# A retention, routing and two-MLP kernel: every routing product with a stationary operand of 128 columns and 128 rows

## The chip, the core and the metric

The kernel runs on one core of a Trainium2 chip. The metric is the device time of one execution in microseconds (us), lower is better. The time shown of a kernel is the median of several executions; the profile is of one further execution, whose own time stands beside it.

Engines: PE (TensorE, matrix products), PEld (the loads of PE's stationary operand, which may run ahead of the products), DVE (VectorE), ACT (ScalarE), POOL (GpSimd), SP (SyncE, which here issues DMAs and loads one register per expert).

## What is computed

Three stages follow each other: a retention layer (attention with a decay instead of a softmax), a mixture of eight experts with a greedy capacity, and a dense MLP. The cut reference:

```python
# retention: B, H, S, D = 4, 8, 576, 64
scores = scale * np.matmul(q, k.transpose(0, 1, 3, 2))
ret = scores * Dmat[None]                  # gamma[h] ** (i - j) for i >= j
x = (ret @ v) as [2304 tokens, 512]
# routing: 8 experts, capacity 288 tokens each
logits = x @ w_gate
for idx in np.argsort(-logits.flatten()):
    tok, e = idx // 8, idx % 8
    if assigned[tok] >= 0 or counts[e] >= 288: continue
    assigned[tok] = e; counts[e] += 1
# experts, F = 1024
out[mask_e] = np.maximum(x[mask_e] @ w1[e], 0) @ w2[e]
# dense MLP, DFF = 2048
h = x @ w_in; g = h * np.tanh(softplus(h)); return g @ w_out
```

## The kernel before, in words

**Retention** (`attention`) goes over 18 tiles of 128 tokens. PE, DVE and POOL follow an order written by hand; SP loads `qk` and `kv` of a tile (512 KB each) three tiles ahead. The constants come by a few DMAs between the first loads; one of them is `cst` (L273), which holds the 128x128 identity and a triangle. POOL fills the constants of the routing at the start (`routing_setup`).

**Routing.** The greedy assignment is done expert by expert: in each of eight rounds the expert is found that is filled first, and the logit (threshold) at which it is. The threshold is found digit by digit in six steps over the 32-bit key (`route`, L427 to L450). In a step with m candidates (m is 63, 63, 31, 31, 31, 32) DVE writes marks `G` (L427; tokens on 128 partitions, 18 tiles by 64 columns, m of them used), PE adds up 18 products `pF` with `G[:, t, :m]` as the stationary operand and the one-hot choice `oh` (8 columns) as the moving one (L445), DVE compares with the capacity (`sat`, L366), PE multiplies with `digit` (L450, m rows by 128 columns), and DVE takes the maximum (L411) and goes on to the next step. A step of the first round's first digit stands in L305. After six steps two small products (`before` and `oneb`, 128x128, L474 and L475) number the chosen tokens.

Then `tokens` builds the list of the expert's tokens: DVE writes a one-hot matrix `ohb` (L587, 18 tiles by 96 columns) in two halves of nine tiles, PE multiplies each half by `R` (18 products `pI`, 96 columns stationary, 6 moving, L595), DVE turns the sums into indices (`chosen`, L599), and POOL gathers the rows with indirect DMAs. The rows are transposed on PE (`mmx`, L628) and split into high and low parts.

**Experts** (`experts`): per expert 96 products `mma` and 96 `mmb` of 128x288 (L771), each value as a sum of three products of split parts. While the products of expert i run, the rounds of the next ones go on. **Order**: from the first round's second step on, a planner (`run_tasks`) chooses the order of PE, DVE, POOL, ACT and SP in the program with costs and priorities written into the `yield` lines; on the chip every engine then runs its list in that order and waits with semaphores. So six times there is a batch of 18 routing products on PE between two runs of `mma` or `mmb`. In the first round there are no expert products yet, and PE fills some of its waiting time with `warm` products (L781). The weights of `w_in` and `w_out` are converted piece by piece on ACT, DVE and POOL in the same stretch (`narrow`, tiles `words`, `dw`).

**Dense MLP** (`tiles`): six tiles of 384 tokens, `mmc` (L987) and `po` (L1048), until the end.

Of the kernel before, what the change touches and what calls it, by code (L numbers as in the profile page):

```python
# [17 lines left out]
P = 128  # L18
# [63 lines left out]
FC, FCN = _layout([("ident", P), ("tri", P)])  # L82
# [6 lines left out]
def constants():  # L89
    p = np.arange(P)  # L90
    f = np.zeros((P, FCN), np.float32)
    f[:, FC["ident"]] = np.eye(P)
    f[:, FC["tri"]] = p[:, None] <= p[None, :]
# [30 lines left out]
    return {"consts": f, "decays": d, "masks": m.reshape(P, 2, -1), "rconsts": r, "iconsts": c}  # L124
# [8 lines left out]
class Kernel:  # L133
# [3 lines left out]
    def attention(self):  # L137
# [6 lines left out]
        cst = persist.tile([P, FCN], F32, name="cst")  # L144
        self.ident = ident = cst[:, FC["ident"]]
        self.tri = cst[:, FC["tri"]]
        self.L = L = persist.tile([P, NT, E], F32, name="L")
        with ExitStack() as st:
# [124 lines left out]
            nc.sync.dma_start(cst, a["consts"])  # L273
# [21 lines left out]
            G = self.rw.tile([P, NT, 64], BF16, name="G")  # L295
            self.chosen = self.rw.tile([GB, E, 3], I32, name="chosen", bufs=1)
            pF = self.psum("pF", [64, E])
# [16 lines left out]
    def routing_setup(self):  # L314
# [14 lines left out]
        nc.gpsimd.memset(self.open, 1.0)  # L329
        self.tok = pr.tile([P, NT], I32, name="tok")  # L330

    def routing_consts(self):
# [8 lines left out]
        nc.vector.tensor_tensor(self.before, self.tri, self.ident, op=ALU.subtract)  # L341

# [14 lines left out]

    def reached(self, choice, G, ts):

        m, n = WIDTHS[0], ts.stop - ts.start  # L360
        self.nc.vector.tensor_tensor(G[:, ts, :m], choice[0][:, ts, None].to_broadcast([P, n, m]),
                                     self.rc[:, None, RC["first"]].to_broadcast([P, n, m]), op=ALU.is_ge)

    def saturated(self, pF, m):
        sat = self.rw.tile([64, E], BF16, name="sat")
        self.nc.vector.tensor_scalar(sat[:m], pF[:m, :], float(CAP), None, op0=ALU.is_ge)  # L366
        return sat

    def route(self):
# [8 lines left out]
        for i in range(E):  # L378
# [26 lines left out]
            for s in range(6):  # L405
                m = WIDTHS[s]
                if s or i:
# [18 lines left out]
                    G = rw.tile([P, NT, 64], BF16, name="G")  # L426
                    v.tensor_tensor(G[:, :, :m], key[:, :, None].to_broadcast([P, NT, m]),  # L427
# [15 lines left out]
                    pF = self.psum("pF", [64, E])  # L443
# [666 lines left out]
```

## Time and profile before

| | |
|---|---|
| median of 3 runs | 813.99 us (812.19 to 814.79) |
| the profiled execution | 809.8 us, its span 808.0 us |
| PE busy | 766.4 us, 95% of the span |
| DVE busy | 668.5 us, 83% |
| ACT, POOL busy | 413.2 us and 464.4 us |
| granted PE clock over the span | 0.98 of full |

Stages of the span: retention 0 to 84 us, the first round of the routing 84 to about 104 us, waiting for the first weights and rows until 125 us, experts with the other rounds 125 to about 340 us, the last expert and the start of the dense MLP 340 to 460 us, the dense MLP to 808 us.

How to read the rows: a line of a timeline is start, duration, engine, line, operation, output<-inputs, shapes and count; in square brackets the idle time of the engine just before and what ended it. A row that merges several instructions (x18) goes from the start of the first to the end of the last. A line of a window table is its length, then busy us and number of instructions of PE, PEld, DVE, ACT and POOL, then the granted clock of PE (1.00 is 2.4 GHz, 0.50 is 1.2 GHz), the busy share of the DMA engines, and GB/s. Starts on PE are when the instruction is handed to the array, so that what costs time in a dense stretch is the distance from one start to the next.

### The profile page before, as it was taken

How to read it: one execution, taken by the hardware profiler on the slowest of the kernel's cores; microseconds unless marked ns; L12 is line 12 of the kernel's file. 1: busy time of each engine (PE TensorE's matmuls, PEld its weight loads, DVE VectorE, ACT ScalarE, POOL GpSimd, SP SyncE). 2: the span in 40 equal slices, each digit the busy share in tenths (PEclk: the TensorE clock that was granted, in tenths of full speed). 3: DMA queues.
4: the chain of work that ended last, by engine and by line, in shares of the span. 5: the costliest groups of instructions: out<-in, count | busy, mean ns of one | idle time of the engine just before them, and what ended most of it. 6: DMA issues, size and time to landing. Idle time of an engine off the chain costs nothing.

```text
span 808.0 us, 16171 instructions
## 1 busy us (share of the span) xinstructions
PE 766.4 (95%) x6184; PEld 688.3 (85%) x6184; DVE 668.5 (83%) x1089; ACT 413.2 (51%) x781; POOL 464.4 (57%) x402
## 2 busy tenths in 40 slices
PE   7999479999999999799899899999999999999996
PEld 5898338898999989799898788898899988999985
DVE  2444687897988888696698999989998998998993
ACT  1233115556555565575664455555556556555552
POOL 3653035779797796340166776657466566655644
PEclk9999789999999999899999999999999999999999
DMA  9993165888888887986700010001001001000001
GB/s 342 408 354 129 41 208 184 265 264 283 252 290 251 299 265 229 331 270 231 247 1 21 20 40 21 12 21 47 2 20 40 19 21 40 20 1 13 27 1 39
DMA packets 61117, 112.52 MB, mean 139 GB/s; under 512 B 4848, under 2 KB 33008, under 8 KB 61040
## 3 DMA queue, kind: packets, MB, share of 16 engines
q1 hardware_dynamic: 44816, 74.00, 26.8%
q10 hardware_dynamic: 13248, 28.06, 10.4%
q0 software_dynamic: 2976, 9.44, 3.6%
q8 instruction: 48, 0.79, 0.4%
q14 instruction: 29, 0.24, 0.1%
HBM read 88.93 MB, written 22.54 MB: 138 GB/s over the span
## 4 chain that ended last, share of the span: by engine, by line
PE 59%; DVE 8%; DMA 2%; POOL 2%; issue 2%; ACT 1%; SPq 0%; POOLq 0%; ACTq 0%; DVEq 0%
PE mmc L987 23%; PE po L1048 21%; PE mmb L771 7%; PE mma L771 7%; DVE q L1017 2%; DMA st<-w 1%; PE pF L445 1%; DVE hl L797 1%; DVE ohb L587 1%; DVE wlo L560 1%; DVE G L427 1%; DMA st<-w_out 1%; POOL n L1019 1%; POOL gl L1029 1%; DVE n L1012 1%
## 5 line engine op out<-in xcount | busy, mean ns | idle before, releaser
L1017 DVE RECIPROCAL q<-q 128x384 f32<-128x384 f32 x96 | 244.3, 2545 | 11.3 <-ACT q L1015 9.7
L1019 POOL TENSOR_TENSOR n<-n,q 128x384 f32<-128x384 f32 x96 | 99.3, 1034 | 140.3 <-DVE q L1017 137.7
L1029 POOL TENSOR_TENSOR gl<-n,gh 128x384 fp32r<-128x384 f32 x96 | 105.4, 1098 | 50.5 <-ACT gh L1027 50.1
L987 PE MATMUL mmc<-yl,whi 128*128 128x384 f32 x384 | 130.2, 339 | 4.3 <-POOL yl L947 2.5
L987 PE MATMUL mmc<-yh,whi 128*128 128x384 f32 x384 | 130.0, 339 | 0.6 <-ACT yh L944 0.5
L987 PE MATMUL mmc<-yh,wlo 128*128 128x384 f32 x384 | 129.7, 338 | 0.0
L560 POOL TENSOR_TENSOR wlo<-st,whi 128x1024 fp32r<-128x1024 f32 x49 | 116.9, 2400 | 13.1 <-ACT whi L557 12.4
L1048 PE MATMUL po<-whi,gh 128*128 128x512 f32 x288 | 114.0, 396 | 0.0
L1048 PE MATMUL po<-whi,gl 128*128 128x512 f32 x288 | 113.9, 395 | 0.0
L1048 PE MATMUL po<-wlo,gh 128*128 128x512 f32 x288 | 113.3, 393 | 0.0
L1005 ACT ACTIVATE s<-mmc 128x384 f32<-128x384 f32 x96 | 47.1, 491 | 122.2 <-PE mmc L987 119.2
L1012 DVE SCALAR_TENSOR_TENSOR n<-s 128x384 f32<-128x384 f32 x96 | 103.3, 1076 | 2.1 <-ACT s L1005 1.2
L557 ACT CAST whi<-st 128x1024 fp32r<-128x1024 f32 x80 | 82.0, 1043 | 40.5 <-DMA st<-w 31.6
L771 PE MATMUL mma<-xh,whi 128*128 128x288 f32 x256 | 77.5, 303 | 3.0 <-DVE xl L620 3.0
L987 PEld LDWEIGHTS mmc<-yl,whi 128*128 128x128 f32 x384 | 72.1, 188 | 9.5 <-POOL yl L947 3.4
L771 PE MATMUL mmb<-hl,whi 128*128 128x288 f32 x256 | 77.9, 304 | 0.0
L771 PE MATMUL mmb<-hh,whi 128*128 128x288 f32 x256 | 77.4, 302 | 0.0
L771 PE MATMUL mmb<-hh,wlo 128*128 128x288 f32 x256 | 77.3, 302 | 0.0
L987 PEld LDWEIGHTS mmc<-yh,whi 128*128 128x128 f32 x384 | 72.1, 188 | 5.5 <-ACT yh L944 1.5
L771 PE MATMUL mma<-xh,wlo 128*128 128x288 f32 x256 | 76.7, 300 | 0.0
L771 PE MATMUL mma<-xl,whi 128*128 128x288 f32 x256 | 76.6, 299 | 0.0
L987 PEld LDWEIGHTS mmc<-yh,wlo 128*128 128x128 f32 x384 | 72.2, 188 | 0.0
(146 smaller groups left out, 1541.2 us busy)
## 6 DMA issues: line engine op xcount, KB each, us to landing
st<-w SPq DMA_DIRECT2D x64, 512.0 KB, 5.7
qk<-qk SPq DMA_DIRECT2D x18, 512.0 KB, 7.9
kv<-kv SPq DMA_DIRECT2D x18, 512.0 KB, 8.1
std<-w_out ACTq DMA_DIRECT2D x15, 512.0 KB, 5.1
std<-w_in ACTq DMA_DIRECT2D x14, 512.0 KB, 5.3
x_scratch<-xs SPq DMA_DIRECT2D x18, 256.0 KB, 4.1
y_scratch<-y ACTq DMA_DIRECT2D x32, 144.0 KB, 3.9
yt<-y_scratch SPq DMA_DIRECT2D x22, 192.0 KB, 2.4
```

The costliest lines, as they stand in the source:

```text
L427: v.tensor_tensor(G[:, :, :m], key[:, :, None].to_broadcast([P, NT, m]), T[:, None, :].to_broadcast([P, NT, m]), op=ALU.is_ge)
L445: nc.tensor.matmul(pF[:m, :], G[:, t, :m], oh[:, t, :], start=(t == 0), stop=(t == NT - 1))
L557: self.nc.scalar.copy(dst[0], st)
L560: (self.nc.vector if lo.engine == DVE else self.nc.gpsimd).tensor_tensor(dst[1], st, dst[0].bitcast(F32), op=ALU.subtract)
L771: self.nc.tensor.matmul(bank[1][:, :CAP], al if h == 2 else ah, bl if h == 1 else bh, start=(first and j == h == 0), stop=(last and j == n ...
L987: self.nc.tensor.matmul(bank[1][:, :TILE], (wl if h == 2 else wh)[:, c, cs], x[c][h == 1], start=(c == h == 0), stop=(c == HP - 1 and h == 2))
L1005: nc.scalar.activation(s, p, AF.Sigmoid)
L1012: v.scalar_tensor_tensor(u, s, 2.0, s, op0=ALU.subtract, op1=ALU.mult)
L1017: v.reciprocal(q, q)
L1019: nc.gpsimd.tensor_tensor(u, u, q, op=ALU.mult)
L1029: nc.gpsimd.tensor_tensor(gl, u, gh.bitcast(F32), op=ALU.subtract)
L1048: nc.tensor.matmul(po[j], (gl if h == 2 else gh)[:, js], (wl if h == 1 else wh)[:, f % 2], start=(f == h == 0), stop=(f == DFF // P - 1 an ...
```

## The change

Each stationary operand of a routing product becomes 128 columns and 128 rows:

- `G` is now one of two fixed tiles of 18 x 64 + 64 columns, filled with zeros once and used in turn (`marks_of`). The product of tile t reads columns 64 t to 64 t + 128: its own 64 and those of tile t + 1. Beyond its own m marks it reads marks of the next tile or of earlier steps; the surplus rows of `pF` (now 128) hold sums that nothing needs.
- `sat` is compared over 128 rows; `digit` has 128 rows and is zero beyond m, so that the surplus counts nothing.
- `ohb` is a fixed tile with 32 more columns (zero). The product of tile t reads columns 96 t to 96 t + 128; the surplus rows of `pI` are not read.
- `ident` and `tri` become two DMAs instead of one (`cst`).
- The costs of the planner stay as they are, and so does the order of the instructions on each engine after the start.

```diff
-        pF = self.psum("pF", [64, E])
+        pF = self.psum("pF", [P, E])
...
-                nc.tensor.matmul(pF[:WIDTHS[0], :], G[:, i, :WIDTHS[0]], choice[2][:, i, :], start=(i == 0), stop=(i == NT - 1))
-            self.first_step = choice, self.saturated(pF, WIDTHS[0])
+                nc.tensor.matmul(pF, G[:, i * 64:i * 64 + P], choice[2][:, i, :], start=(i == 0), stop=(i == NT - 1))
+            self.first_step = choice, self.saturated(pF)
...
-        self.digit = pr.tile([64, 6, P], BF16, name="digit")
+        self.digit = pr.tile([P, 6, P], BF16, name="digit")
+        nc.gpsimd.memset(self.digit, 0.0)
         for i, s in enumerate(SHIFTS):
-            nc.gpsimd.memset(self.digit[:, i, :], float(2 ** s))
+            nc.gpsimd.memset(self.digit[:WIDTHS[i], i, :], float(2 ** s))
...
+        self.G = [self.rw.tile([P, NT * 64 + 64], BF16, name=f"G{i}", bufs=1) for i in range(2)]
+        self.ohb = self.rw.tile([P, NT * GB + P - GB], BF16, name="ohb", bufs=1)
+        for g in self.G:
+            nc.gpsimd.memset(g, 0.0)
+        nc.gpsimd.memset(self.ohb[:, NT * GB:], 0.0)
...
+    def marks_of(self):
+        self.G.reverse()
+        return self.G[0]
...
-        sat = self.rw.tile([64, E], BF16, name="sat")
-        self.nc.vector.tensor_scalar(sat[:m], pF[:m, :], float(CAP), None, op0=ALU.is_ge)
+        sat = self.rw.tile([P, E], BF16, name="sat")
+        self.nc.vector.tensor_scalar(sat, pF, float(CAP), None, op0=ALU.is_ge)
...
-                        nc.tensor.matmul(pF[:m, :], G[:, t, :m], oh[:, t, :], start=(t == 0), stop=(t == NT - 1))
+                        nc.tensor.matmul(pF, G[:, t * 64:t * 64 + P], oh[:, t, :], start=(t == 0), stop=(t == NT - 1))
...
-                nc.tensor.matmul(pD, self.digit[:m, s, :], sat[:m], start=True, stop=True)
+                nc.tensor.matmul(pD, self.digit[:, s, :], sat, start=True, stop=True)
...
-                nc.tensor.matmul(pI, ohb[:, t], R[:, t].rearrange("p g c -> p (g c)"), start=(t == 0), stop=(t == NT - 1))
+                nc.tensor.matmul(pI, self.ohb[:, t * GB:t * GB + P], R[:, t].rearrange("p g c -> p (g c)"), start=(t == 0), stop=(t == NT - 1))
...
-            nc.sync.dma_start(cst, a["consts"])
+            nc.sync.dma_start(self.ident, a["ident"])
+            self.tri = one.tile([P, P], F32, name="tri")
+            nc.sync.dma_start(self.tri, a["tri"])
```

Two places show what moves. The first is PE in the sixth round (the list of the fifth expert after the first), from the ninth product of the first half of `ohb` to the start of the second half; three expert products `mma` stand between the halves. LDWEIGHTS is the load of the stationary operand, and in brackets is what it waits for. Before:

```order
L595 LDWEIGHTS ohb
L595 MATMUL pI_4746<-R,ohb 96x6
L771 MATMUL mma_4731<-xh,whi 128x288
L771 MATMUL mma_4731<-xl,whi 128x288
L771 MATMUL mma_4731<-xh,wlo 128x288
L595 LDWEIGHTS ohb [waits DVE_49]
```

With the change, the same place:

```order
L603 LDWEIGHTS ohb [waits DVE_49]
L603 MATMUL pI_4713<-R,ohb 128x6
L779 MATMUL mma_4698<-xh,whi 128x288
L779 MATMUL mma_4698<-xl,whi 128x288
L779 MATMUL mma_4698<-xh,wlo 128x288
L603 LDWEIGHTS ohb
```

The order is the same; the wait for DVE's second half of `ohb` moved from the tenth load to the ninth, since the ninth now reads 32 columns of tile nine, and with that ahead of the three expert products. The same is so in all eight rounds.

The second place is the start of SP's list, the DMAs of constants and first tiles; `DMAHW` is one of eight semaphores that the DMAs take in turn, each waiting for the one eight before it. Before:

```order
L272 DMA both<-both 128x288
L273 DMA cst<-consts 128x256
L174 DMA qk<-qk 128x1024 [waits DMAHW0_49]
L176 DMA kv<-kv 128x1024 [waits DMAHW1_49]
L275 DMA mask_83<-masks 128x1024 [waits DMAHW2_49]
L174 DMA qk<-qk 128x1024 [waits DMAHW3_49]
```

With the change:

```order
L266 DMA both<-both 128x288
L267 DMA ident<-ident 128x128
L269 DMA tri<-tri 128x128 [waits DMAHW0_49]
L168 DMA qk<-qk 128x1024 [waits DMAHW1_49]
L170 DMA kv<-kv 128x1024 [waits DMAHW2_49]
L271 DMA mask_83<-masks 128x1024 [waits DMAHW3_49]
```

There is one DMA more, of the same bytes in all, and the loads of tile 2 and the next ones wait for a DMA that was issued one place later.

## Rows read from the trace of the kernel before

**Rows 1.** The page's part 4, the chain of work that ended last.
```profile
PE 59%; DVE 8%; DMA 2%; POOL 2%; issue 2%; ACT 1%; SPq 0%; POOLq 0%; ACTq 0%; DVEq 0%
```

**Rows 2.** Window table: one cycle of an expert in the middle.
```profile
250.00:284.00 34.00, 33.95 (x338) 31.48 (x336) 29.22 (x95) 19.86 (x34) 27.91 (x16) 1.00 0.85 276
```

**Rows 3.** Window table: a piece of the first round.
```profile
92.00:94.00 2.00, 0.61 (x17) 0.45 (x17) 1.43 (x6) 0.00 (x0) 0.00 (x0) 0.50 0.00 0
```

**Rows 4.** Timeline of PE in the first round: a batch of 63 columns, one of 31.
```profile
90.76 1.12 PE L445 MATMUL pF<-oh,G 128*63 128x8 bf16 x18 [2.53 <-DVE known L432]
...
93.56 0.65 PE L445 MATMUL pF<-oh,G 128*31 128x8 bf16 x18 [1.26 <-DVE known L432]
```

**Rows 5.** Groups by shape, PEld, 90 to 102 us: count, busy us, mean ns, idle before.
```profile
L445 PEld LDWEIGHTS <-G 128*31 128x31 bf16 x54 | 1.7, 104 | 4.9 <-DVE known L432 4.9
L445 PEld LDWEIGHTS <-G 128*63 128x63 bf16 x18 | 1.0, 155 | 2.6 <-DVE known L432 2.6
...
L450 PEld LDWEIGHTS <-digit 31*128 31x128 bf16 x3 | 0.3, 98 | 0.1
```

**Rows 6.** Timeline, 103.2 to 104.4 us: two products with 128x128 in a row.
```profile
103.80 0.16 PE L474 MATMUL pP<-scan,before 128*128 128x2 bf16 x1 [2.24 <-DVE scan L471]
103.80 0.10 PEld L475 LDWEIGHTS <-oneb 128*128 128x128 bf16 x1 [2.21 <-issue]
103.83 0.16 PE L475 MATMUL pP<-scan,oneb 128*128 128x1 bf16 x1
```

**Rows 7.** Groups by shape, PEld, 125 to 303 us.
```profile
L445 PEld LDWEIGHTS <-G 128*31 128x31 bf16 x288 | 8.2, 94 | 3.6 <-DVE steps L437 2.3 <-DVE known L432 1.2
L445 PEld LDWEIGHTS <-G 128*63 128x63 bf16 x180 | 6.6, 114 | 2.4 <-DVE G L427 1.4 <-DVE known L432 1.0
...
L475 PEld LDWEIGHTS <-oneb 128*128 128x128 bf16 x5 | 0.5, 100 | 0.0
```

**Rows 8.** Timeline of PE, sixth round: the two halves of ohb, then batches.
```profile
280.32 0.53 PE L595 MATMUL pI<-R,ohb 128*96 128x6 bf16 x9
...
281.25 0.57 PE L595 MATMUL pI<-R,ohb 128*96 128x6 bf16 x9
281.67 0.38 PE L771 MATMUL mmb<-hh,whi 128*128 128x288 f32 x1
...
282.49 0.75 PE L445 MATMUL pF<-oh,G 128*63 128x8 bf16 x18
283.17 0.40 PE L771 MATMUL mmb<-hl,whi 128*128 128x288 f32 x1
...
290.10 0.61 PE L445 MATMUL pF<-oh,G 128*31 128x8 bf16 x18
290.63 0.40 PE L771 MATMUL mmb<-hl,whi 128*128 128x288 f32 x1
```

**Rows 9.** Timeline of DVE at the same place.
```profile
280.14 1.05 DVE L587 TENSOR_TENSOR ohb<-sc,rc 128x864 bf16<-128x864 f32 x1
281.11 1.33 DVE L427 TENSOR_TENSOR G<-sc,rc 128x1134 bf16<-128x1134 f32 x1
...
283.63 0.75 DVE L740 SCALAR_TENSOR_TENSOR dw<-std,ic,words 128x512 uint32<-128x512 uint32 x1
284.29 0.17 DVE L411 TENSOR_REDUCE sc<-pD 128x1 uint32<-128x8 f32 x1
...
286.64 0.14 DVE L432 TENSOR_TENSOR known<-known,sc 128x1 uint32<-128x1 uint32 x1
```

**Rows 10.** Timeline of PE in the eighth round: the second half of ohb.
```profile
319.53 0.57 PE L595 MATMUL pI<-R,ohb 128*96 128x6 bf16 x9
```

**Rows 11.** Timeline of DVE in the eighth round.
```profile
319.39 0.75 DVE L737 TENSOR_SCALAR words<-words,ic 128x512 uint32<-128x512 uint32 x1
320.13 0.16 DVE L599 TENSOR_REDUCE chosen<-pI 96x3 int32<-96x6 f32 x1
```

**Rows 12.** Timeline of POOL at the start.
```profile
1.90 0.90 POOL L324 MEMSET digit<- 64x128 bf16 x6
...
11.83 1.04 POOL L187 TENSOR_TENSOR ks<-kv,dec 128x512 f32<-128x512 f32 x1 [8.69 <-DMA kv<-kv]
```

**Rows 13.** Window table: the DMAs at the start.
```profile
8.00:10.00 2.00, 0.50 (x20) 0.26 (x12) 1.46 (x3) 0.00 (x0) 0.00 (x0) 1.00 1.02 406
```

More of the change, by code (lines that the diff above doesn't have):

```diff
@@ L79, in _layout @@
     return out, o
-FC, FCN = _layout([("ident", P), ("tri", P)])
 DC, DCN = _layout([("gk", NT * H), ("gs", NT * HP), ("gq", HP * P)])
@@ L90, in constants @@
     p = np.arange(P)
-    f = np.zeros((P, FCN), np.float32)
-    f[:, FC["ident"]] = np.eye(P)
-    f[:, FC["tri"]] = p[:, None] <= p[None, :]
     gamma = 1.0 - 2.0 ** (-5.0 - np.arange(H, dtype=np.float64))
@@ L143, in attention @@
         self.sc = self.right.enter_context(tc.tile_pool(name="sc", bufs=1, space=PSUM, side="right")).tile([P, 512], F32, name="sc")
-        cst = persist.tile([P, FCN], F32, name="cst")
-        self.ident = ident = cst[:, FC["ident"]]
-        self.tri = cst[:, FC["tri"]]
+        self.ident = persist.tile([P, P], F32, name="ident")
         self.L = L = persist.tile([P, NT, E], F32, name="L")
@@ L294, in attention @@
             self.psum = lambda name, shape: ps.tile(shape, F32, name=name, tag="pS" if name == "pF" else "pA", bufs=1 if name == "pF" else 2)
-            G = self.rw.tile([P, NT, 64], BF16, name="G")
+            G = self.marks_of()
             self.chosen = self.rw.tile([GB, E, 3], I32, name="chosen", bufs=1)
-            pF = self.psum("pF", [64, E])
+            pF = self.psum("pF", [P, E])
             early, late = slice(0, t - 1), slice(t - 1, NT)
@@ L425, in route @@
                         T = Tu[:, :m].bitcast(F32)
-                    G = rw.tile([P, NT, 64], BF16, name="G")
-                    v.tensor_tensor(G[:, :, :m], key[:, :, None].to_broadcast([P, NT, m]),
+                    G = self.marks_of()
+                    v.tensor_tensor(G[:, :NT * 64].rearrange("p (t m) -> p t m", m=64)[:, :, :m], key[:, :, None].to_broadcast([P, NT, m]),
                                     T[:, None, :].to_broadcast([P, NT, m]), op=ALU.is_ge)
@@ L442, in route @@
                     at = yield PE, 90 + 17 * m, [at], 0
-                    pF = self.psum("pF", [64, E])
+                    pF = self.psum("pF", [P, E])
                     for t in range(NT):
-                        nc.tensor.matmul(pF[:m, :], G[:, t, :m], oh[:, t, :], start=(t == 0), stop=(t == NT - 1))
+                        nc.tensor.matmul(pF, G[:, t * 64:t * 64 + P], oh[:, t, :], start=(t == 0), stop=(t == NT - 1))
                     at = yield DVE, 155, [at], 0
-                    sat = self.saturated(pF, m)
+                    sat = self.saturated(pF)
                 at = yield PE, 105, [at], 0
                 pD = self.psum("pD", [P, E])
-                nc.tensor.matmul(pD, self.digit[:m, s, :], sat[:m], start=True, stop=True)
+                nc.tensor.matmul(pD, self.digit[:, s, :], sat, start=True, stop=True)
             at = yield DVE, 2100, [at], 0
@@ L581, in tokens @@
         v.tensor_scalar(R[:, :, :, 1], g, self.rc[:, RC["base"]][:, NT:], None, op0=ALU.mult)
-        ohb = rw.tile([P, NT, GB], BF16, name="ohb", bufs=1)
+        ohb = self.ohb[:, :NT * GB].rearrange("p (t b) -> p t b", b=GB)
         halves = [slice(0, NT // 2), slice(NT // 2, NT)]
@@ L598, in tokens @@
         with nc.allow_low_precision(reason="small integers"):
-            v.tensor_reduce(idx, pI.rearrange("p (g c) -> p g c", c=2), AX.X, ALU.add)
+            v.tensor_reduce(idx, pI[:GB].rearrange("p (g c) -> p g c", c=2), AX.X, ALU.add)
         self.banks[nI] = self.listed[i] = at
```

7 lines of the change are left out of this document (4 added, 3 removed).

## The prediction

> **What bounds the kernel now.** I read the chain of waits first, then a table of windows, then timelines of PE and DVE around the lines that the diff touches. The chain is PE for 59% of the span and DVE for 8% [rows 1]; it can be followed back only to 199 us. In a cycle of one expert PE is busy 33.95 of 34 us at the full clock of 2.4 GHz [rows 2]. So from 125 to 318 us a product that costs PE less is worth its time, unless DVE holds the next step back. The first round of the routing (84 to 104 us) is something else: PE and DVE wait for each other, nothing runs beside it, and the granted clock there is 0.50, that is 1.2 GHz [rows 3]. There each ns of a batch lies on the path.
>
> **What a load of 128 columns costs.** This decides the sign, so I take it first. In a batch of 18 load and product pairs, PE is paced by the loads: at 1.2 GHz the batch of 63 columns takes 1.12 us, that of 31 columns 0.65 us [rows 4]. The durations of the loads follow: 104 ns for 31 columns, 155 for 63, but 98 for `digit`, which has 128 columns already [rows 5]. At 2.4 GHz it is 94, 114 and, for `oneb` with 128 columns, 100 ns [rows 7]. And at 1.2 GHz the products of `before` and `oneb` start at 103.80 and 103.83 us with the load of `oneb` between them, and the second takes no longer than the first [rows 6]. So in bf16 a load of 128 columns costs what one of 31 does, and one of 63 columns costs more. I take a batch of 128 columns at the 31-column one's price. `digit` had that price with 31 rows, so its new rows bring nothing.
>
> A rule of the Trainium skill bears on this: "TensorE: Matmul & The Clock Gate", section "Weight-path perf modes — Fast Weight Load (FWL) and DoubleRow", states that a load of exactly 128 columns that is not fp32 is read in wider pieces over four paths, in theory four times as fast for fp8 (of bf16 it puts two elements in a piece), and measured about twice as fast on trn2. The trace agrees with four rather than with two; the rival below with half the gain is what two would give. The same page, section "LDWEIGHTS (loading the stationary operand)", speaks against the change: its formula, columns / 1.2 ns, knows no such exception and makes the load of 128 columns about 107 ns; by that every batch gets longer, which is the last rival.
>
> **The change part by part.** (1) *First round.* One batch of 63 columns goes from 1.12 to 0.65 us: **-0.47 us**. The other batch of 63 (L305) stood mostly beside DVE's work, its last two products are worth some 0.05 us. The four batches of 31 and 32 columns stay. What follows (the first weights and rows) is waited for from here, so this lasts. Between -0.55 and -0.4.
>
> (2) *Batches of the later rounds.* At 2.4 GHz a batch of 63 costs 283.17 - 282.49 = 0.68 us of PE, one of 31 columns 290.63 - 290.10 = 0.53 us [rows 8]: -0.15 us for each of the two batches in a round, nothing for the other four.
>
> (3) *The list of tokens.* Nine products of 96 columns cost 281.67 - 281.25 = 0.42 us [rows 8]; at the 31-column price, 0.53 / 18 = 0.03 each, they cost 0.27. But the first half now waits at its ninth product for DVE's second half of `ohb`, and behind it stand the expert products that used to fill that time. In the row, DVE ends that half at 280.14 + 1.05 = 281.19 [rows 9] and PE starts the second half at 281.25, just in time. With the change PE starts the first half at 280.32, is through eight pairs at 280.56, and stands still for 0.69 us until 281.25. Then come the ninth pair (0.03), the three expert products that stood between (281.25 - 280.32 - 0.42 = 0.51 us), and the second half (0.27): 282.06 instead of 281.67, so **+0.4 us** instead of -0.3. The pattern is the same in five rounds (the third to the seventh); in the second and the eighth two products stand between and it is +0.3; in the first, `warm` products stand there and it costs nothing.
>
> (4) *What of (2) and (3) reaches the end.* In the same cycle DVE goes from 280.14 to 286.78 without a pause that PE could shorten: `ohb`, `G`, the conversion steps `words` and `dw`, the maximum at 284.29, the next `G`, `known` [rows 9]; PE starts the second batch of 63 right behind that. So PE, late by 0.4, loses a small wait of 0.1 before the first batch (`G` ends at 282.44, PE starts at 282.49), saves 0.15 in it and is 0.15 late after it; DVE wants the result only at 284.29, behind `dw`, so that this hides; a wait of some 0.05 before 286.78 goes too; and the second batch saves 0.15. The 31-column batches that follow are PE's own and unchanged. Sum of a round: +0.4 - 0.1 - 0.15 - 0.05 - 0.15 = **about 0**. Bounds: -0.15 (the late half hides wholly, only the batch behind `known` gains) to +0.4 (nothing is gained back), for the five rounds -0.75 to +2.0. The second round (PE +0.3 and -0.3) 0, from -0.3 to +0.3.
>
> (5) *Eighth round.* `chosen` starts when `words` ends, at 320.13, while the second half ends at 319.53 + 0.57 = 320.10 [rows 10, 11]. PE starts that half some 0.5 us later (the ninth pair and two expert products come first) and ends it 0.15 sooner: `chosen` **+0.3 us**, and behind it in DVE's list the splits that free the places for the last expert's weights. Between 0 and +0.4.
>
> (6) *Start.* POOL writes 768 columns of zeros, two times 1216 and 32. By `digit`, 0.90 us for 768 columns [rows 12], this is 3.8 us more; POOL then waits 8.69 us for the load of a `kv` tile anyway. **0**; without that cover it would be 3.8. SP issues the loads of tile 2 and the next ones a place later. The DMAs run at 406 GB/s with a busy share of 1.02 meanwhile [rows 13], so that bytes, not the time of issue, set when they land: **0**, at most one load of 512 KB, 1.3 us. `sat` over 128 rows instead of 63 stays one instruction of 8 columns: 0, and not above its 0.15 us.
>
> Sum: -0.47 + 0 + 0.3 = -0.2 us. On the profiled execution of 809.8 us that is 809.6; this execution lies 4.2 us below the median of the runs, 814.0, and on that scale the forecast is **813.8 us**. From the bounds: -0.55 - 0.75 - 0.3 = -1.6 and -0.4 + 2.0 + 0.3 + 0.4 + 1.3 = +3.6, so 812.4 to 817.6, and with the spread of a run (812.19 to 814.79, that is 1.3) 811.1 to about 818.
>
> **The rivals.** *Half the gain* (slower): a load of 128 columns in a stream costs what one of 64 does; single loads in the rows could hide that by running ahead. The batches of 63 then gain nothing, those of 31 and 32 columns lose. First round: 4 x 0.47 = 1.9 us. Six later rounds: 4 batches x 0.15 = 0.6 each on PE, 3.6 us. The wait at the ninth product is then not gained back: +0.4 in five rounds, 0.3 in two, 2.6. Together +8.1: **822 us**. It becomes slower than no change where a 128-column load in a batch costs over about 3 ns more than a 31-column one. Against it: 98 against 104 ns, and 155 for 63 columns at the same clock [rows 5].
>
> *No wait, all gained* (faster): the ninth product doesn't hold PE, and what PE saves all reaches the end: -0.5, 12 batches x 0.15 = -1.8, 14 halves x 0.15 = -2.1, together -4.4: **809.6 us**. For it: PE is dense [rows 2]. Against it: the order has the wait in every round, and DVE ends only 0.06 us before PE's start of the second half [rows 8, 9].
>
> *It doesn't do what it says* (slower by far): 128 columns take the time of 128 columns. From 31 to 63 columns a pair at 1.2 GHz gets longer by (1.12 - 0.65) / 18 / 32 = 0.8 ns for a column, at 2.4 GHz by (0.68 - 0.53) / 18 / 32 = 0.26 ns. First round: 4 x 18 x 97 x 0.8 ns + 18 x 65 x 0.8 ns = 6.5 us; six rounds of 4 x 18 x 97 x 0.26 + 2 x 18 x 65 x 0.26 ns = 2.4 us, 14.5 us, and the wait of 2.6: about +24, **838 us**. The load of `digit` speaks against it.
>
> **How the numbers follow.** A measurement of this kernel can tell 0.3%, 2.4 us, from no change. The forecast has 0.78, half the gain 0.11, all gained 0.08, not what it says 0.03. Faster: 0.08 and a little of the forecast's low end, 0.10. Slower: 0.11 + 0.03 and 0.04 of the forecast's high end, 0.18. Same: 0.72. The range goes from 809.5 (it takes in most of "all gained") to 818; left out are most of the two slow rivals and the tails, under 0.2.
>
> **What the profile after would show.** A batch of what was 63 columns in the first round at 0.65 us, at full clock 0.53 from start to start, the batches of 31 unchanged: (1) and (2). PE idle for 0.4 to 0.7 us ahead of the ninth product of each first half, ended by DVE `ohb`: (3). The second batch of each round still started by `known`: (4). I am wrong if the batches that had 31 columns get longer, if POOL or the loads of tile 2 come late at the start, or if the idle time at the ninth product shows up at the end of a cycle.

## The result and the profile after

The changed kernel takes **806.46 us** (median of 6 runs, 804.62 to 810.0), the kernel before 813.15 in the same comparison (6 runs): ratio 0.991, 95% interval 0.9887 to 0.9932. That is 6.7 us faster, where 813.8 us and no measurable difference was forecast, and below the lower end of the range. The profiled execution took 804.62 us, its span is 802.9 us, 5.1 less than the 808.0 before.

The first round went as forecast. PE's two batches of [rows 4] and the loads of marks of [rows 5]:

```profile
90.76 0.64 PE L453 MATMUL pF<-oh,G 128*128 128x8 bf16 x18 [2.53 <-DVE known L440]
...
93.10 0.64 PE L453 MATMUL pF<-oh,G 128*128 128x8 bf16 x18 [1.27 <-DVE known L440]
```

```profile
L453 PEld LDWEIGHTS <-G 128*128 128x128 bf16 x90 | 2.8, 105 | 9.6 <-DVE known L440 9.6
```

The batch of 63 columns went from 1.12 to 0.64 us, and the next one starts 0.46 earlier (93.56 before). At the full clock, the loads from 125 to 298 us (the place of [rows 7]) take 96 ns instead of 94 and 114:

```profile
L453 PEld LDWEIGHTS <-G 128*128 128x128 bf16 x558 | 16.0, 96 | 8.7 <-DVE known L440 5.9 <-DVE G L435 1.1
...
L603 PEld LDWEIGHTS <-ohb 128*128 128x128 bf16 x90 | 3.3, 96 | 5.6 <-DVE ohb L595 5.1
```

What was not forecast shows in the dense rounds. First PE's timeline of the kernel **before** in the sixth round, around one `digit` product (an expert product by itself starts 0.13 us after the one ahead):

```profile
283.67 0.30 PE L771 MATMUL mmb<-hl,whi 128*128 128x288 f32 x1
283.90 0.18 PE L450 MATMUL pD<-sat,digit 63*128 63x8 bf16 x1
284.00 0.40 PE L771 MATMUL mmb<-hh,wlo 128*128 128x288 f32 x1
284.24 0.29 PE L771 MATMUL mmb<-hh,whi 128*128 128x288 f32 x1
```

And **after**, the list of tokens, a `digit` product and a batch of marks in the same round (the place of [rows 8]):

```profile
275.56 0.35 PE L603 MATMUL pI<-R,ohb 128*128 128x6 bf16 x8
276.89 0.18 PE L603 MATMUL pI<-R,ohb 128*128 128x6 bf16 x1 [0.97 <-DVE ohb L595]
276.93 0.38 PE L779 MATMUL mma<-xh,whi 128*128 128x288 f32 x1
...
277.41 0.38 PE L603 MATMUL pI<-R,ohb 128*128 128x6 bf16 x9
277.65 0.38 PE L779 MATMUL mmb<-hh,whi 128*128 128x288 f32 x1
...
284.38 0.29 PE L779 MATMUL mmb<-hh,whi 128*128 128x288 f32 x1
284.51 0.18 PE L458 MATMUL pD<-sat,digit 128*128 128x8 bf16 x1
284.55 0.38 PE L779 MATMUL mmb<-hl,whi 128*128 128x288 f32 x1
284.77 0.29 PE L779 MATMUL mmb<-hh,wlo 128*128 128x288 f32 x1
...
286.10 0.29 PE L779 MATMUL mmb<-hh,whi 128*128 128x288 f32 x1
286.23 0.61 PE L453 MATMUL pF<-oh,G 128*128 128x8 bf16 x18
286.70 0.38 PE L779 MATMUL mmb<-hl,whi 128*128 128x288 f32 x1
286.92 0.30 PE L779 MATMUL mmb<-hh,wlo 128*128 128x288 f32 x1
```

Read the starts, not the durations. `digit` of 63 rows starts 0.23 us behind the expert product ahead of it, the next product 0.10 behind it, the one behind that 0.24 later: 0.57 in all. With 128 rows it is 0.13, 0.04 and 0.22: 0.39. Over all such places between expert products (medians in us; for the entry of marks and for the halves of the list, where waits mix in, the usual value without one; the sum adds the rounded parts):

| PE work between expert products | into it | its start to the next | next to the one behind | sum |
|---|---|---|---|---|
| before: 18 marks of 63 columns | 0.23 | 0.68 | 0.24 | 1.15 |
| before: 18 marks of 31 or 32 | 0.23 | 0.54 | 0.24 | 1.01 |
| after: 18 marks of 128 | 0.13 | 0.47 | 0.22 | 0.82 |
| before: `digit`, 31 to 63 rows | 0.23 | 0.10 | 0.24 | 0.57 |
| after: `digit`, 128 rows | 0.14 | 0.04 | 0.22 | 0.40 |
| before: 9 of `ohb`, 96 columns | 0.13 | 0.39 | 0.22 | 0.74 |
| after: 9 of `ohb`, 128 columns | 0.13 | 0.24 | 0.22 | 0.59 |

The length of a merged row (first start to last end) helps to read the second column: the batch of 31 columns at 290.10 in [rows 8] is 0.61 us long, and so is the batch of 128 columns at 286.23 above. Read from the single starts, the 17 distances inside a batch are 25 ns each (the first one is longer) with 31 or 32 columns and with 128, and 33 with 63; what differs is the step from the last product of the batch to the expert product behind it, 96 ns with 31 columns and 25 with 128.

So an operand of 31 to 63 rows or columns among full ones cost PE 0.09 us on the way in and 0.08 to 0.09 on the way back (some 0.07 to the next product, 0.02 to the one behind it), and 96 columns cost nothing of the kind. A batch of 63 columns saves 0.13 us inside as well. A round (two batches of 63, four of 31 or 32, six `digit`) is 2 x 0.33 + 4 x 0.19 + 6 x 0.17 = 2.4 us cheaper on PE, where the prediction had 0.30.

About a third of it was left at the end of the rounds. The waits of PE that end with DVE, 126 to 318 us (total, times, longest), before and after:

```profile
PE pF L445 <- DVE known L432: 1.8, 3, 0.7
PE pI L595 <- DVE ohb L587: 0.3, 1, 0.3
```

```profile
PE pI L603 <- DVE ohb L595: 5.0, 7, 1.0
PE pF L453 <- DVE known L440: 4.0, 6, 1.2
PE pD L458 <- DVE sat L374: 0.8, 3, 0.3
PE pF L453 <- DVE G L435: 0.6, 2, 0.3
```

The two timelines can be set against each other exactly: from the first transposition of gathered rows (123.97 us before, 123.02 after) to the list of the eighth round (318.70, 313.58), the same 1073 expert products lie in 194.73 and 190.56 us. All distances from one start to the next, by what stands between:

| distance | before | after | difference |
|---|---|---|---|
| expert product to expert product (911) | 121.14 | 121.77 | +0.6 |
| marks: into, inside, first product behind | 35.23 | 31.97 | -3.3 |
| `digit`: the same | 17.42 | 13.31 | -4.1 |
| list: the same | 10.10 | 12.95 | +2.9 |
| the rest | 10.84 | 10.56 | -0.3 |
| sum | 194.73 | 190.56 | -4.2 |

I call this stretch the rounds. By the prices above, its 32 batches or so (10 of 63 columns), 32 `digit` products and 13 half lists should have become 7.5, 5.4 and 2.0 us cheaper, 15 in all. The marks lack 4.2 of it and `digit` 1.3, by longer waits for DVE and a few places at a lower clock; the list turned a gain of 2.0 into a loss of 2.9, which is the wait at the ninth product. The 0.95 us by which the stretch starts earlier comes on top; 0.44 of it is the first round, and the rest may be chance, since in the profiles of the further kernels (the one with 127 columns apart) the stretch starts anywhere from 122.3 to 125.1 us. So a kernel's rounds are compared by their length below.

The +0.6 comes of a short fall of the clock (granted 0.50 from 278.49 to 281.90 us). Window table after, a piece of the cycle of [rows 2] right behind the 0.97 us wait at 276.89:

```profile
276.00:278.00 2.00, 1.11 (x15) 1.04 (x16) 2.00 (x2) 0.39 (x2) 0.00 (x0) 1.00 0.75 274
278.00:280.00 2.00, 2.00 (x28) 1.78 (x26) 1.98 (x6) 2.00 (x4) 0.94 (x1) 0.62 0.39 147
280.00:282.00 2.00, 2.00 (x11) 2.00 (x11) 1.81 (x6) 1.58 (x3) 1.61 (x2) 0.52 0.74 134
```

Products start 0.24 us apart there instead of 0.13, and some 1.4 us are lost, 0.9 of them between expert products. The same wait of 0.97 us at 210.42 and 243.66 was not followed by a fall.

The last expert's first product starts 5.4 us earlier, and this lead stays to the end (its last product starts at 391.6 instead of 396.8, the span is 5.1 shorter):

```profile
334.44 0.40 PE L771 MATMUL mma<-xh,whi 128*128 128x288 f32 x1 [2.95 <-DVE xl L620]
```

```profile
329.00 0.40 PE L779 MATMUL mma<-xh,whi 128*128 128x288 f32 x1 [2.44 <-DVE xl L628]
```

### The profile page after: what moved, and what is told of

Its sections match the earlier page's. It is cut to its first block, busy times and chain, and to the rows that moved or that the text cites. A ratio compares the mean times of both kernels' runs of the same rounds, so it can differ in the third digit from the quotient of the medians.

```text
span 802.9 us, 16174 instructions
## 1 busy us (share of the span) xinstructions
PE 751.5 (94%) x6184; PEld 678.4 (85%) x6184; DVE 669.9 (83%) x1089; ACT 413.0 (51%) x781; POOL 466.9 (58%) x406
## 4 chain that ended last, share of the span: by engine, by line
PE 61%; DVE 24%; issue 5%; DMA 4%; ACT 2%; POOL 2%; SPq 0%; ACTq 0%; POOLq 0%; DVEq 0%
PE mmc L995 19%; PE po L1056 18%; PE mmb L779 7%; PE mma L779 5%; DVE q L1025 4%; DVE G L435 2%; DVE n L1020 2%; PE pX L246 2%; PE pT L232 2%; DMA qk<-qk 2%; PE pA L195 2%; DVE hl L805 2%; PE pF L453 2%; DVE ohb L595 2%; DMA st<-w 1%
## 5 line engine op out<-in xcount | busy, mean ns | idle before, releaser
L568 POOL TENSOR_TENSOR wlo<-st,whi 128x1024 fp32r<-128x1024 f32 x49 | 117.0, 2400 | 10.8 <-ACT whi L565 10.0
L1020 DVE SCALAR_TENSOR_TENSOR n<-s 128x384 f32<-128x384 f32 x96 | 103.2, 1075 | 2.1 <-ACT s L1013 1.2
```

What stands on the lines that cost most here:

```text
L568: (self.nc.vector if lo.engine == DVE else self.nc.gpsimd).tensor_tensor(dst[1], st, dst[0].bitcast(F32), op=ALU.subtract)
L1020: v.scalar_tensor_tensor(u, s, 2.0, s, op0=ALU.subtract, op1=ALU.mult)
```

## The experiments

The theory: the gain is PE's changing between full operands and those of 31 to 63 rows or columns, in the marks and in `digit`; the wait at the ninth product takes part of it back, and DVE becomes the bound of the rounds. The rivals: only the shorter loads of the batches count, or the cheap load itself is what saves the entry; the ninth product's wait is harmless, or is all that holds back the rest.

Beside the times, one table, made from the profiles as the one above: the length of the rounds (first transposition to the list of the eighth round) and its parts, in us. The 911 distances from expert product to expert product are the same work in each; above 121.4 there, the clock fell. What a part costs holds the waits in it. Three runs are left out: 127 columns (rounds of 207.37 us), the kernel before with less on DVE (196.75, at half the clock for 6.8 us), and the planner's costs (187.97, in another order).

| kernel | rounds | expert to expert | marks | `digit` | list | rest |
|---|---|---|---|---|---|---|
| before | 194.73 | 121.14 | 35.23 | 17.42 | 10.10 | 10.84 |
| after | 190.56 | 121.77 | 31.97 | 13.31 | 12.95 | 10.56 |
| after, once more | 189.11 | 120.92 | 32.02 | 12.94 | 12.94 | 10.29 |
| after, `digit` back to m rows | 191.87 | 120.71 | 30.39 | 18.18 | 11.86 | 10.73 |
| before, `digit` alone | 191.69 | 121.37 | 37.32 | 12.32 | 10.16 | 10.52 |
| after, marks alone | 190.38 | 120.74 | 30.82 | 18.03 | 10.26 | 10.53 |
| before, list alone | 194.73 | 120.73 | 34.30 | 17.26 | 11.83 | 10.61 |
| after, wait moved | 189.05 | 120.79 | 34.08 | 13.13 | 10.51 | 10.54 |
| after, less on DVE | 191.13 | 124.93 | 28.31 | 12.50 | 14.85 | 10.54 |
| after, both | 186.61 | 121.66 | 29.83 | 12.12 | 12.46 | 10.54 |

The two profiles of the changed kernel differ by 1.5 us, 0.85 of it at the lower clock.

**`digit` back to m rows.** Changed kernel, with

```diff
-                nc.tensor.matmul(pD, self.digit[:, s, :], sat, start=True, stop=True)
+                nc.tensor.matmul(pD, self.digit[:m, s, :], sat[:m], start=True, stop=True)
```

> The changed kernel with one part undone: the product of digit and sat takes m rows again (63, 31 or 32) instead of 128; marks and lists keep 128 columns. Theory A (change of operand size): PE loses time whenever it goes from a full stationary operand to one of at most 64 rows or columns and back, whatever the load costs. Then a digit product between two expert products takes 0.57 us again (start of the one before to start of the second one behind, 0.23 + 0.10 + 0.24) instead of 0.40; 36 of them stand between expert products, so 6 us more of PE and 2 to 5 us more of time than the changed kernel: 808 to 812 us. Theory B (price of the load alone): 128 rows cost what 31 do, so the digit product stays at 0.40 and the time at 806.

Measured: 807.87 us, ratio 0.994 (0.9923 to 0.9956). PE's timeline:

```profile
285.88 0.29 PE L779 MATMUL mmb<-hh,whi 128*128 128x288 f32 x1
286.11 0.18 PE L458 MATMUL pD<-sat,digit 63*128 63x8 bf16 x1
286.22 0.40 PE L779 MATMUL mmb<-hl,whi 128*128 128x288 f32 x1
286.46 0.30 PE L779 MATMUL mmb<-hh,wlo 128*128 128x288 f32 x1
```

The old distances 0.23, 0.11 and 0.24 are back, with the same load of 128 columns: the number of rows decides, not the load. In the table `digit` costs 18.18 us instead of 13; as marks and list wait less by 2.7, the rounds are 1.3 to 2.8 us longer than in the two profiles of the changed kernel. By medians the time is 1.4 us longer, just below the 808 to 812 expected, and the intervals do not separate the two.

**127 instead of 128.** Changed kernel, marks and `digit` one short of full:

```diff
-                        nc.tensor.matmul(pF, G[:, t * 64:t * 64 + P], oh[:, t, :], start=(t == 0), stop=(t == NT - 1))
+                        nc.tensor.matmul(pF[:127], G[:, t * 64:t * 64 + 127], oh[:, t, :], start=(t == 0), stop=(t == NT - 1))
...
-                nc.tensor.matmul(pD, self.digit[:, s, :], sat, start=True, stop=True)
+                nc.tensor.matmul(pD, self.digit[:127, s, :], sat[:127], start=True, stop=True)
```

> The changed kernel with marks of 127 columns (and 127 rows of digit and sat) instead of 128. Both theories say that the load is no longer a cheap one: a batch of 18 goes from 0.47 us to about 1.0 (127 columns at the slope from 63 to 96 columns of the kernel before, 0.34 to 0.48 ns a column, 0.055 to 0.06 a pair). They differ at the entry. Theory A: 127 columns count as a full operand, so PE goes from an expert product to the batch in 0.13 us, and the digit product stays at 0.40. Theory B (what made the entry slow was a load that isn't cheap and so can't run ahead): entry 0.23 again. Time by both well over the changed kernel, 36 batches by 0.55 are 20 us of PE: 815 to 826 us.

Measured: 834.08 us, ratio 1.023 (1.0173 to 1.0287), where 815 to 826 was expected: a miss in the size. The expectation left out the first round, which is 7.3 us longer from its first batch to the products of `before`, and the granted clock, which is 0.50 from 126 to 143 us. A `digit` product and a batch of marks on PE, the loads, and a batch of the first round:

```profile
290.24 0.29 PE L779 MATMUL mma<-xl,whi 128*128 128x288 f32 x1
290.38 0.18 PE L458 MATMUL pD<-sat,digit 127*128 127x8 bf16 x1
290.42 0.38 PE L779 MATMUL mma<-xh,wlo 128*128 128x288 f32 x1
290.63 0.29 PE L779 MATMUL mma<-xh,whi 128*128 128x288 f32 x1
```

```profile
232.73 0.29 PE L779 MATMUL mmb<-hh,whi 128*128 128x288 f32 x1
232.86 1.17 PE L453 MATMUL pF<-oh,G 128*127 128x8 bf16 x18
233.90 0.38 PE L779 MATMUL mmb<-hl,whi 128*128 128x288 f32 x1
```

```profile
L453 PEld LDWEIGHTS <-G 128*127 128x127 bf16 x511 | 36.1, 149 | 5.7 <-DVE known L440 4.7 <-DVE G L435 0.6 <-issue 0.2
```

```profile
94.61 2.08 PE L453 MATMUL pF<-oh,G 128*127 128x8 bf16 x18 [1.27 <-DVE known L440]
```

This separates the two savings. With 127 rows or columns the way in stays at 0.13: 127 counts as full. But the batch takes 1.04 us instead of 0.47, 59 ns from product to product instead of 25; at 1.2 GHz, in the first round, it is 107 ns instead of 27. So the short load is there at 128 columns and not at 127. It is also the rival "it doesn't do what it says", run, if with the cheaper change of operand: that forecast +24 us, and it is 2.3%, some 19.

**`digit` alone.** Kernel before, `digit` and `sat` over 128 rows, rows of `sat` beyond m zero from the start:

```diff
-                nc.tensor.matmul(pD, self.digit[:m, s, :], sat[:m], start=True, stop=True)
+                nc.tensor.matmul(pD, self.digit[:, s, :], sat, start=True, stop=True)
```

> The kernel before with one part of the change alone: digit and sat get 128 rows (zero beyond m); marks keep 63, 31 and 32 columns, the list 96. Theory A: a digit product between expert products falls from 0.57 to 0.40 us, 36 of them, 6 us of PE; of that 2 to 5 us reach the end: 808 to 811 us. Theory B: no change, 813.

Measured: 811.03 us, ratio 0.9967 (0.995 to 0.9985). `digit` costs 5.1 us less in the rounds, 2.1 of it come back as waits of the marks, 3.0 are left. What the prediction held to bring nothing makes the kernel faster by itself.

**Marks alone.** Changed kernel with `digit` and `sat` back to m rows and the list back to 96 columns:

```diff
-                nc.tensor.matmul(pI, self.ohb[:, t * GB:t * GB + P], R[:, t].rearrange("p g c -> p (g c)"), start=(t == 0), stop=(t == NT - 1))
+                nc.tensor.matmul(pI[:GB], self.ohb[:, t * GB:t * GB + GB], R[:, t].rearrange("p g c -> p (g c)"), start=(t == 0), stop=(t == NT - 1))
```

> The changed kernel with only the marks at 128 columns: digit takes m rows and the list of tokens 96 columns, as before the change. By theory A (change of operand size) a batch between expert products costs 0.82 us from the start of the one before to the start of the second one behind, instead of 1.16 (63 columns) and 1.01 (31 and 32): 12 x 0.34 + 24 x 0.19 = 8.6 us less of PE than before the change; digit products 0.57 and the list's nine products 0.39, as before, and no idle time ahead of a ninth product. Of PE's gain a third to a half reaches the end in the runs so far (1.4 to 2.2 of 6 us for digit alone): 809 to 811 us. By theory B (load alone; 63 columns gain 0.15 us, 31 nothing) 1.8 us less of PE: 812 to 813.

Measured: 806.43 us, ratio 0.9904 (0.9871 to 0.9937); 809 to 811 was expected, so this is a miss. The marks alone bring as much as the whole change: 4.4 us less in the marks, and little loss elsewhere (0.6 at `digit`). PE waits 3.1 us for `known`, 0.7 for `sat` and 0.3 for `ohb`.

**List alone.** Kernel before with `ohb` 128 columns wide:

> The kernel before with one part of the change alone: the list's stationary operand has 128 columns, so that the ninth product waits for DVE's second half; marks and digit stay. The operand had 96 columns, for which PE changed from an expert product in 0.13 us already, so theory A gives nothing beyond the load: nine products in 0.24 us instead of 0.39. Against that PE stands idle for 0.5 to 1.0 us ahead of the ninth product in seven rounds. By the prediction's part (3) PE is 0.3 to 0.4 us later a round, 2.6 us in all: 814 to 816 us. If DVE sets the end of those stretches, no change: 813.

```diff
-                nc.tensor.matmul(pI, ohb[:, t], R[:, t].rearrange("p g c -> p (g c)"), start=(t == 0), stop=(t == NT - 1))
+                nc.tensor.matmul(pI, self.ohb[:, t * GB:t * GB + P], R[:, t].rearrange("p g c -> p (g c)"), start=(t == 0), stop=(t == NT - 1))
```

Measured: 812.18 us, ratio 0.9995 (0.997 to 1.0019), where 814 to 816 was expected. PE does stand at the ninth product:

```profile
PE pI L597 <- DVE ohb L589: 3.7, 6, 1.0
PE pF L447 <- DVE known L434: 1.4, 3, 0.6
```

but the rounds are as long as before, 194.73 us: the list costs 1.7 more, the marks 0.9 less, since they come later and wait less for DVE, and the rest is spread over the other parts. So the 814 to 816, worked out from part (3) of the prediction, were a miss, and the other case, "If DVE sets the end of those stretches, no change", held.

**The wait moved away.** Changed kernel, halves of 8 and 10 products, so that the ninth stands behind the expert products:

```diff
-            for t in range(ts.start, ts.stop):
+            for t in (range(NT // 2 - 1) if ts.start == 0 else range(NT // 2 - 1, NT)):
```

> The changed kernel with the ninth product of the list moved from the first half's run to the second half's (8 and 10 products instead of 9 and 9), so that the wait for DVE's second half of the one-hot matrix stands behind the expert products again. If the wait costs what the traces say (PE idle 0.46 to 0.97 us ahead of the ninth product in seven rounds, 5.0 us in all, expert products that could have run in it), 2 to 3 us are gained: 803 to 804 us, and PE's idle time at the list falls under 1 us. If DVE holds the rounds back anyway, PE waits elsewhere and the time stays at 806.

Measured: 805.93 us, ratio 0.9905 (0.9871 to 0.9939): no measurable difference to the changed kernel, though the wait for `ohb` falls from 5.0 us to 1.4. The table says where it went: against the changed kernel once more the list costs 2.4 us less, the marks 2.1 more, and the rounds are as long (189.05 and 189.11). PE gets to the next steps sooner and waits there for DVE's `known` and `G`, 5.5 us instead of 4.4. So the ninth product's wait is not what holds back the rest; it is one of the places where PE waits for DVE. The last expert is no sooner done either (its last product starts at 392.0 us, against 391.6 and 392.2): PE goes on with it 0.7 us earlier than after (328.31 against 329.00), but has waited longer, 4.08 us instead of 2.44, while ACT waits for the load of the last expert's weights; and the granted clock, 0.50 behind that wait, stays so for 10.2 us instead of 6.8:

```profile
325.58 1.04 ACT L565 CAST whi<-st 128x1024 fp32r<-128x1024 f32 x1 [4.36 <-DMA st<-w]
```

**The changed kernel once more**, in the same comparison as the marks alone, the list alone and the planner's costs:

> The changed kernel once more, beside the others on the same chip, in five rounds, for its distance to them: 806 us, ratio 0.991. Both theories say the same.

Measured: 807.41 us, ratio 0.9912 (0.9881 to 0.9944), span 806.2; `ohb` again 5.0 us in seven waits. In this profile no ninth product is followed by a fall of the clock.

**The planner's costs.** As with the wait moved, and the planner told what the products now cost:

```diff
-                    at = yield PE, 90 + 17 * m, [at], 0
+                    at = yield PE, 480, [at], 0
...
-                at = yield PE, 105, [at], 0
+                at = yield PE, 40, [at], 0
...
-            for t in range(ts.start, ts.stop):
+            for t in (range(NT // 2 - 1) if ts.start == 0 else range(NT // 2 - 1, NT)):
```

> The changed kernel with the ninth product moved (8 and 10) and with two of the planner's costs on PE set near to what the traces show: a batch of marks 480 ns instead of 90 + 17 m (617 to 1161), a digit product 40 instead of 105. The planner then puts fewer expert products between a batch and the step that follows it. If what is left over of PE's gain goes to waits for DVE (PE idle for known and G 4 to 6 us in the rounds), a plan nearer to the times can move expert products into them: 802 to 805 us. If the last expert's weights and the DMA set the end after the eighth round, the time stays at 805 to 806.

Measured: 809.92 us, ratio 0.9954 (0.9933 to 0.9974), by medians 2.5 to 4 us slower than with the old costs, where 802 to 805 was expected; its ten runs (808.49 to 811.01) all lie above the six of the changed kernel in the same comparison (804.02 to 807.95). The rounds are even shorter, 187.97 us, but the last expert's rows are waited for 4.59 us (until 328.64) and its last product starts at 395.9. The trace shows what the order costs there: twelve products of the dense MLP now stand among the last expert's `mmb`, and PE waits 8.1 us for their inputs, where the changed kernel comes to them behind the expert and waits 2.8; the granted clock is 0.50 from 380.56 to 390.80 us:

```profile
380.19 0.44 PE L995 MATMUL mmc<-yh,whi 128*128 128x384 f32 x1 [3.80 <-ACT yh L952]
384.93 0.69 PE L995 MATMUL mmc<-yl,whi 128*128 128x384 f32 x1 [4.30 <-DVE yl L955]
```

**DVE relieved.** One instruction in each conversion of weight pieces left out (32 of 0.75 us on DVE), in the changed kernel, in the kernel before, and together with the wait moved:

```diff
-            v.tensor_scalar(w, w, ic[:, IC["three"]], None, op0=ALU.logical_shift_left)
```

> The changed kernel without DVE's shift of `words` (32 instructions of 0.75 us, part of the conversion of w_in and w_out, which are wrong then), all else in the same order; most of them stand between the steps of the routing. If what PE saved in the rounds went into waits for DVE (PE idle 2.1 us in the rounds before the change, 10.4 us with it), then these waits shrink to 4 to 6 us, and 4 to 6 us are gained up to the eighth round; the last expert's weights may take 1 to 2 us of it: 801 to 804 us. If PE or the DMA sets the rounds, nothing: 806.

> The kernel before, without the same 32 DVE instructions. There PE is idle only 2.1 us in the rounds, so if PE sets them, taking 24 us off DVE gives 0 to 2 us: 811.5 to 813.5, clearly less than it gives the changed kernel. If DVE set the rounds before the change too, it gives as much as there: 808 to 810.

> The changed kernel with the ninth product moved behind the expert products (8 and 10) and without DVE's 32 shifts of `words` (so that w_in and w_out come out wrong). In the run without `words` alone the waits for known fell and those at the ninth product grew, and the granted clock fell to 0.50 for some 7 us behind one of them. If PE's gain was held up by DVE at these two places, and the ninth wait also costs clock, then PE is idle 2 to 5 us in the rounds instead of 10.3, no fall of the clock stands in them, and the eighth round's list comes at 308 to 310 us instead of 312.6 to 313.6: 801 to 803 us, or 804 if the last expert's weights take the rest. If the rounds are held by something else, 804 to 806.

Measured: 804.24 us (0.9894, 0.9845 to 0.9943; 801 to 804 was expected), 811.54 (0.9984, 0.996 to 1.0008) and 802.38 (0.989, 0.9839 to 0.9941). PE's waits in the changed kernel with less on DVE, and with both:

```profile
PE pI L603 <- DVE ohb L595: 6.6, 9, 1.0
PE pF L453 <- DVE known L440: 1.1, 2, 0.6
```

```profile
PE pI L603 <- DVE ohb L595: 3.3, 6, 1.2
PE pF L453 <- DVE known L440: 1.1, 2, 0.6
...
```

With less on DVE the waits for `known` go from 4.0 to 1.1 us, and the marks cost 3.7 us less than after; PE then comes to the list earlier and waits there, 6.6 instead of 5.0, and two waits in a row (1.00 us until 205.91, 0.97 until 207.24) are followed by 6.8 us at half the clock. The same happens behind the waits of 0.43 us until 274.33 and 0.97 until 275.66; the two falls together take 4 us back between expert products. The first one:

```profile
206.00:208.00 2.00, 1.03 (x21) 0.86 (x22) 2.00 (x3) 0.04 (x1) 0.00 (x0) 1.00 0.79 256
208.00:210.00 2.00, 2.00 (x30) 1.85 (x27) 1.18 (x5) 2.00 (x3) 0.80 (x1) 0.53 0.40 143
210.00:212.00 2.00, 2.00 (x10) 1.85 (x10) 1.55 (x5) 1.58 (x4) 1.39 (x3) 0.50 0.44 111
```

With both, the rounds are 186.61 us, the shortest of all, and the last product of the last expert starts at 387.8. The time is within the 801 to 803 us expected, but in part by luck: the kernel before took only 810.56 us in the same comparison, and 811.93 in that of the other two, instead of 813.15. The forecast that no fall of the clock would stand in the rounds was a miss: the waits of 1.19, 0.47 and 0.20 us from 204.4 to 208.2 are followed by 3.4 us at half the clock. The kernel before gains nothing measurable from the same relief (its profile fell to half the clock for 6.8 us in the rounds, so that its parts are not compared). By the ratios to the kernel before, the changed kernel gains some 1.3 us from less DVE work and 1.6 from both, and the intervals overlap with its own: that DVE holds the rounds after the change rests on the traces, not on the times.

## Why the prediction was wrong

**The price of a load of 128 columns: right.** 96 ns against 94 for 31 columns and 114 for 63, a batch in the first round 0.64 us whatever its columns had been, and from product to product 25 ns at the full clock with 31 columns as with 128. "Half the gain" and "it doesn't do what it says" are out; the run with 127 columns shows what the latter would have cost, and bears out four rather than two as well: 107 ns from product to product at 1.2 GHz, where 128 columns take 27. "No wait, all gained" had the direction, but not the reason: the wait is there, and the gain is one that it didn't count.

**(1), the first round: right.** -0.47 was forecast for the batch, -0.48 measured; the end of the steps (103.80 before) comes 0.44 earlier.

**(2), the later batches: the step that failed.** It took the distance from a batch's start to the next product as its whole price, and gave 128 columns the 0.53 us of 31: -0.15 for the batches of 63, "nothing for the other four". Missing were the way in (0.23 instead of 0.13) and the way back, which an operand of 31 to 63 columns costs and one of 128 doesn't: the 0.53 us held 0.07 of the way back, which was taken for a price of the load, and the rest stands outside it. The batch is 0.82 against 1.15 and 1.01: -0.33 and -0.19, so 1.4 us a round, not 0.3. With "its new rows bring nothing" for `digit` it failed in the same way: the load's duration (98 ns) is indeed the same, and yet each of six `digit` products in a round costs 0.17 us less, 1.0 more. The evidence was in the trace of before: the list of 96 columns starts 0.13 us behind an expert product (280.19 to 280.32 us), the batches of 31 and 63 and every `digit` 0.23. I looked at durations of loads and at the distance on one side of a batch, never at that on the other. By the prediction's own last paragraph, batches of 31 were to stay "unchanged", at 0.53 from start to start; they went from 0.54 to 0.47 us, all of it at the last step, and that alone would have told it.

A sentence of the Trainium skill, "TensorEngine Tiling (Array Packing)", section "Tiling Modes", bears on this, and I had not weighed it: the array may be cut into tiles of 32, 64 or 128 rows and columns, and changing the mode "drains the TensorE". The traces fit it: 31 to 63 rows or columns cost a change among products of 128x128, 0.09 us in and 0.08 to 0.09 back, and 96 and 127 don't. That a change of this mode is the reason is not shown by them; what they show is the price by size.

**(3), the ninth product: the wait right, its size too small.** 0.69 us of standing was forecast for the sixth round; it is 0.97 there and 0.46 to 0.97 in the seven rounds, each time ended by DVE's `ohb`, 5.0 us in all. From the list's first product to the expert product behind its second half it is 277.65 - 275.56 = 2.09 us instead of 281.67 - 280.32 = 1.35 [rows 8]: +0.7 where +0.4 was forecast.

**(4), what of it reaches the end: right in kind, the sum wrong.** It said that DVE, going through a cycle without a pause, decides what PE keeps. So it is: of 15 us of cheaper PE work 4.2 were left at the eighth round (5.6 in the second profile), mostly since the waits for DVE grew from 2.1 to 10.4 us, 8.3 of the 10.8 lost; waits that the shown duration of the product ahead covers and the fall of the clock come on top. But with 2.4 us a round in (2) in place of 0.3, the sum of the six rounds was not "about 0" but -4.2 to -5.6 us.

**(5), the eighth round: right.** Its ninth product waits 0.47 us (until 314.41) and `chosen` 0.20 us for the second half; `chosen` starts 1.64 us behind the list's first product instead of 1.43, +0.2 where +0.3 was forecast. This is lost in the 5 us by which the whole round comes earlier.

**(6), the start: right.** POOL's fills end at 6.09 us instead of 3.15 (2.9 more; 3.8 was forecast), and its first work on a tile starts at 11.94 instead of 11.83 [rows 12], since it waits for the same load:

```profile
11.94 1.04 POOL L181 TENSOR_TENSOR ks<-kv,dec 128x512 f32<-128x512 f32 x1 [5.84 <-DMA kv<-kv]
```

The first batch of the routing starts at 86.20 against 86.24 (87.15 in the second profile, where the first round itself is as short as in the first).

**Open.** The rounds start 0.95 us earlier after the change, of which the first round explains 0.44. Whether a clock fall follows a wait at the ninth product changes from one execution to the next (once in seven waits in one profile of the changed kernel, never in the other); what decides it was not tried. No run keeps the fixed tiles and the split constants but marks of m columns; that these bring nothing by themselves is argued from the start of the routing and from the distances. None of the versions that compute all of the kernel is measurably faster than the changed one: the marks alone, and the wait moved, equal it.

## What to carry to other kernels

Where small products stand among full 128x128 ones, read the distance to the product ahead and to the two behind, not only the load's duration and the batch: here a stationary operand of 31 to 63 rows or columns cost some 0.17 us of changing to and fro each time, and padding it to 128 removed that and made the bf16 loads no longer. Padding by reading into the neighbour's columns moves waits to an earlier product, so look at what is queued behind that product, and expect the next engine in the loop (here DVE) to take most of the gain. Do the parts one by one: the marks alone brought as much as all of it, `digit` alone less than half, and the list nothing.

## What the runs showed of the hardware

- A bf16 load of 128 columns in a stream costs no more than one of 31, and far less than one of 127: 25 ns from product to product at the full clock for 31 and for 128 columns, 33 for 63, 45 for 96 and 59 for 127; at 1.2 GHz 27 for 31 and for 128, and 107 for 127.
- Among products of 128x128 at 2.4 GHz, whether PE pays for a change of operand follows the size: 96 and 127 columns and 127 rows count as full, 31 to 63 rows or columns don't; with rows the load has 128 columns either way. Sizes from 64 to 95 were not run.
- In an otherwise dense stretch a wait of 0.97 us was in one execution followed by 3.4 us at 1.2 GHz and in others by none; two waits in a row were followed by 6.8 us (1.00 and 0.97 us; 0.43 and 0.97 us) and three (1.19, 0.47 and 0.20 us) by 3.4 us; and in the kernel before with less on DVE a fall of 6.8 us from 214.68 stands 1.7 us behind a wait of only 0.26 us.
